# Layer norm by centring the activation and one accumulating variance pass, decay folded per 256 tokens, new prologue and drain

## The chip, the cores and the metric

The kernel runs on one core of a Trainium2 chip. The profile shows four compute engines: PE (TensorE, matrix products), DVE (VectorE), ACT (ScalarE) and POOL (GpSimd). They run side by side (busy for 91, 75, 69 and 66% of one span in the kernel before), each in the order in which the program queues its work. SP only issues DMA transfers here. The kernel keeps its tiles in two on-chip memories, SBUF and PSUM; it has the matrix products written to PSUM.

The metric is the device time of one execution in microseconds (us). Each kernel was run several times. The time of a run is about 1.8 us longer than the span that the profile shows.

## The reference, cut to what matters

```python
q, k, v: (8 batches, 8 heads, 576 tokens, 64)         # float32
rel = pos[:, None] - pos[None, :]
ret = scale * (q @ k.T) * where(rel >= 0, gamma[h] ** rel, 0)     # causal, decaying; no softmax
x = (ret @ v), all heads of a token side by side      # (4608 tokens, 512)
h = x @ w_in                                          # (4608, 1024)
sm = exp(h - max(h)) / sum(exp(h - max(h)))
solu = h * sm
ln = (solu - mean(solu)) / sqrt(var(solu) + 1e-6) * g_ln
out = ln @ w_out                                      # (4608, 512)
```

Two things make the code below easier to read. Layer norm does not change when solu is multiplied by a constant per token, so the kernel drops the division by the sum `se` of the exponentials and adds 1e-6 * se * se to the variance instead (`eps` in the changed kernel). And the attention is done in windows of 256 tokens (2 tiles of 128) with a running state, the decayed sum of k x v, for everything earlier.

## The kernel before: the parts that matter here

The work is 36 token tiles of 128 tokens (index `t`) and 36 half-windows of 4 heads (index `i`). Every operation is listed with its engine, what it needs and what buffers it takes; a list of queue orders per engine, worked out in advance, says in what order each engine runs them. So the program fixes the order of each engine's work, and `h`, the PSUM tile of the first product, has a single buffer.

POOL prepares the attention inputs and the state. All of these read SBUF:

```python
def scale(i, nm, base):                       # q and k: 128x512, times gamma ** position
    t = pools["qk16"].tile([P, 2, 4, D], F16, ...)
    nc.gpsimd.tensor_tensor(out=t..., in0=st[i][nm + "r"], in1=g_of(i, base), op=ALU.mult)
def cast_v(i):                                # v: 128x512
    nc.gpsimd.tensor_copy(out=t, in_=st[i]["vr"])
def state_b(i, c):                            # decay of the state, 128x128
    nc.gpsimd.tensor_tensor(out=d["g"][:, c], in0=d["tt"], in1=g128(i % 2), op=ALU.mult)
def state_cast(i):                            # state to fp16, needed by PE's xy product
    for e in range(2):
        nc.gpsimd.tensor_copy(out=s16[ee[e], :, :, ee[e]], in_=st[i]["g"][ee[e]])
```

The layer norm of a tile. Here `w2c16` is g_ln * w_out with its mean over the 1024 rows taken off once, in the prologue, so that solu itself need not be centred: the weights do it.

```python
def exp_(t):   # ACT; e and the sum of e
    nc.scalar.activation(out=d["e"], in_=d["h"], func=ACT.Exp, accum_out=ws[w]["se"][:, c : c + 1])
def solu(t):   # DVE
    nc.vector.tensor_tensor(out=d["solu"], in0=d["h"], in1=d["e"], op=ALU.mult)
def stats(t):  # DVE
    for half in range(2):
        nc.vector.bn_stats(out=bs[:, half], in_=tk[t]["solu"][:, half * 512 : half * 512 + 512])
    nc.vector.bn_aggr(out=d["mv"][:, c], in_=bs)
    if c:      # once for two tiles
        nc.vector.scalar_tensor_tensor(out=x, in0=d["se"], scalar=1e-6, in1=d["se"],
                                       op0=ALU.mult, op1=ALU.mult)
        nc.vector.tensor_tensor(out=d["x2"], in0=x, in1=d["mv"][:, :, 1], op=ALU.add)
def ln_tp(t):  # PE: 8 transposes of d["solu"], then ACT copies them to lnT
def mm2(t):    # PE: o_ps = sum over c of lnT[:, c].T @ w2c16[:, c]
def w_mean(c), w_center(x):   # prologue: mean of the weights by matmuls (PE), centring (DVE)
```

The softmax here doesn't subtract the row's maximum and nothing guards it: scores larger than these inputs give would overflow.

## Time and profile before

The time is 230.75 us (median of 3 runs, 229.46 to 231.84).

| part of the span (228.9 us) | reading | from |
|---|---|---|
| prologue | first products (L412) start at 19.2, 25.7, 34.9, 40.3 us; the first second product (L475) at 44.1 | starts of the groups in the timeline |
| steady part | one first product every 5.343 us, from the eighth (64.2) to the 33rd (197.7) | the same |
| drain | 17.4 us from the last first product (211.5) to the end | the same |

The busy times of the whole execution, from the page's first part (engine, us, share of the span, number of instructions):

```profile
PE 208.0 (91%) x2964; PEld 122.9 (54%) x2964; DVE 170.7 (75%) x307; ACT 157.6 (69%) x230; POOL 150.9 (66%) x243
```

The same by stretches of time (window view; columns as in its first line, each number in brackets a count of instructions):

```profile
core 0: us, PE busy (x) PEld busy (x) DVE busy (x) ACT busy (x) POOL busy (x), PEclk, DMA share, GB/s
0.00:25.00 25.00, 16.94 (x237) 9.28 (x238) 12.38 (x31) 11.47 (x17) 17.37 (x29) 0.80 0.98 277
25.00:50.00 25.00, 21.08 (x319) 12.39 (x318) 20.92 (x39) 18.14 (x27) 18.29 (x30) 0.93 0.99 280
...
125.00:150.00 25.00, 25.00 (x409) 15.59 (x407) 21.43 (x39) 19.32 (x29) 20.61 (x34) 1.00 0.74 204
150.00:175.00 25.00, 25.00 (x404) 15.45 (x403) 20.88 (x38) 19.43 (x30) 20.76 (x35) 1.00 0.68 180
```

In the steady part PE is busy all the time and nothing else is. DVE and POOL have about 4 of 25 us left each. The page's summary of the chain that ended last agrees (its share by engine):

```profile
PE 70%; DMA 9%; DVE 6%; POOL 5%; ACT 4%; SPq 2%; issue 2%; ACTq 0%; POOLq 0%; DVEq 0%
```

DVE's costliest groups (form, count, busy us, mean ns of one, then the idle time in front of them):

```profile
L438 DVE BATCH_NORM_STATS2 bs<-solu 128x6 f32<-128x512 f16 x72 | 46.0, 680 | 0.1
L432 DVE TENSOR_TENSOR solu<-h_ps,e_sb 128x1024 f16<-128x1024 f32 x36 | 44.0, 1223 | 20.8 <-ACT e_sb L425 20.8
L363 DVE TENSOR_TENSOR ret<-s_ps,masks 128x1024 f16<-128x1024 f32 x36 | 43.7, 1215 | 6.5 <-PE s_ps L330 6.4
```

Note that the large multiplies `solu` and `ret` have one input in PSUM, and that the statistics take one input (0.674 to 0.695 us in all 72). Only tiny instructions of this DVE queue have two inputs in SBUF. What becomes of such an instruction is in the timeline (start, duration, engine, line, what it does):

```profile
59.72 1.04 POOL L258 TENSOR_TENSOR k_1258<-kr,small 128x512 f16<-128x512 f32 x1 [0.27 <-DMA kr<-in_k_dram]
...
60.02 0.76 DVE L446 SCALAR_TENSOR_TENSOR w<-se 128x2 f32<-128x2 f32 x1
...
60.72 1.04 POOL L258 TENSOR_TENSOR q_1320<-qr,small 128x512 f16<-128x512 f32 x1
60.81 0.97 DVE L449 TENSOR_TENSOR w_1255<-w,mv 128x2 f32<-128x2 f32 x1
```

Each of the two DVE instructions handles two numbers per partition and takes 0.11 or 0.16 us when nothing holds it up.

### The profile page before, as it was taken

What the parts mean: (1) busy time and instruction counts of PE and PEld (TensorE: products, weight loads), DVE (VectorE), ACT (ScalarE), POOL (GpSimd) and SP (SyncE); (2) the same over time, 40 slices, a digit from 0 to 9 for tenths busy, and PEclk for the clock granted to TensorE, in tenths of its full rate; (3) what the DMA queues carried; (4) which work ended last, traced back from release to release, by engine and by line L of the source; (5) the groups of instructions that cost most, each with busy time, mean ns of one, the idle gap of its engine ahead of it and who ended that gap; (6) DMA issues with size and microseconds to landing.
All of it is one profiled execution on the core that took longest, in us unless ns stands there. A gap on an engine that the chain in (4) does not pass through costs nothing.

```text
span 228.9 us, 7317 instructions
## 1 busy us (share of the span) xinstructions
PE 208.0 (91%) x2964; PEld 122.9 (54%) x2964; DVE 170.7 (75%) x307; ACT 157.6 (69%) x230; POOL 150.9 (66%) x243
## 2 busy tenths in 40 slices
PE   7577587998989999999999999999999999999961
PEld 2344244565556665655666665666666656654420
DVE  6334778996888898987788798879898989676700
ACT  2165596677678777777777777777777777777621
POOL 3787549868786976978287978797697879201010
PEclk9857979999999999999999999999999999999999
DMA  7999999783992355999776866877855442222243
GB/s 189 329 351 254 299 316 289 207 244 77 282 333 61 103 128 135 272 312 296 196 203 180 210 185 184 240 212 196 224 128 132 122 98 66 63 57 49 47 102 83
DMA packets 66659, 42.64 MB, mean 186 GB/s; under 512 B 5056, under 2 KB 60480, under 8 KB 66624
## 3 DMA queue, kind: packets, MB, share of 16 engines
q1 hardware_dynamic: 66192, 41.96, 66.8%
q8 instruction: 23, 0.38, 0.7%
q10 hardware_dynamic: 432, 0.20, 0.4%
q14 instruction: 12, 0.10, 0.1%
HBM read 32.71 MB, written 9.44 MB: 184 GB/s over the span
## 4 chain that ended last, share of the span: by engine, by line
PE 70%; DMA 9%; DVE 6%; POOL 5%; ACT 4%; SPq 2%; issue 2%; ACTq 0%; POOLq 0%; DVEq 0%
PE o_ps L475 24%; PE h_ps L412 22%; PE xy L295 8%; DMA qr<-in_q_dram 6%; PE tln L461 6%; PE tqk L275 6%; PE s_ps L330 4%; DMA kr<-in_k_dram 3%; DVE solu L432 2%; DVE ret L363 2%; SPq L243 1%; POOL g L385 1%; DVE bs L438 1%; ACT o_sb L482 1%; ACT qkT L283 1%
## 5 line engine op out<-in xcount | busy, mean ns | idle before, releaser
L475 PE MATMUL o_ps<-w2c_120,lnT 128*128 128x512 f16 x288 | 68.3, 380 | 2.0 <-ACT o_sb L482 2.0
L412 PE MATMUL h_ps<-w_in_118,xT 128*128 128x512 f16 x288 | 68.6, 380 | 1.0 <-ACT w_in_118 L582 0.7
L432 DVE TENSOR_TENSOR solu<-h_ps,e_sb 128x1024 f16<-128x1024 f32 x36 | 44.0, 1223 | 20.8 <-ACT e_sb L425 20.8
L425 ACT ACTIVATE e_sb<-h_ps 128x1024 f32<-128x1024 f32 x36 | 36.8, 1024 | 20.5 <-PE h_ps L412 20.3
L363 DVE TENSOR_TENSOR ret<-s_ps,masks 128x1024 f16<-128x1024 f32 x36 | 43.7, 1215 | 6.5 <-PE s_ps L330 6.4
L438 DVE BATCH_NORM_STATS2 bs<-solu 128x6 f32<-128x512 f16 x72 | 46.0, 680 | 0.1
L283 ACT COPY qkT<-tqk 128x1024 f16<-128x1024 f16 x36 | 36.2, 1005 | 10.7 <-PE tqk L275 10.7
L412 PEld LDWEIGHTS <-xT 128*128 128x128 f16 x288 | 27.0, 98 | 27.9 <-issue 2.0
L475 PEld LDWEIGHTS <-lnT 128*128 128x128 f16 x288 | 25.7, 98 | 30.0 <-issue 2.6
L482 ACT ACTIVATE o_sb<-o_ps,rs 128x512 f32<-128x512 f32 x36 | 24.8, 688 | 23.7 <-PE o_ps L475 14.5
L469 ACT COPY lnT<-tln 128x1024 f16<-128x1024 f16 x36 | 36.2, 1004 | 1.8 <-PE tln L461 1.8
L385 POOL TENSOR_TENSOR g<-tt,small 128x128 f32<-128x128 f32 x48 | 19.6, 409 | 25.7 <-DVE tt L381 25.3
L461 PEld LDWEIGHTS <-solu 128*128 128x128 f16 x288 | 19.0, 99 | 8.3 <-DVE solu L432 0.8
L400 ACT CAST xT<-xy 128x512 f16<-128x512 f32 x36 | 21.4, 595 | 2.6 <-DVE g L377 1.5
L461 PE MATMUL tln<-ident,solu 128*128 128x128 f16 x288 | 22.5, 222 | 0.3 <-DVE solu L432 0.3
L381 DVE TENSOR_TENSOR tt<-xy,g 128x128 f32<-128x128 f32 x48 | 13.7, 286 | 7.6 <-ACT xT L400 3.8
L330 PE MATMUL s_ps<-qkT 64*64 64x128 f16 x576 | 15.6, 228 | 2.8 <-ACT qkT L283 2.8
L330 PEld LDWEIGHTS <-qkT 64*64 64x64 f16 x576 | 9.8, 110 | 6.2 <-ACT qkT L283 3.7
L377 DVE TENSOR_TENSOR g<-xy,small 128x128 f32<-128x128 f32 x16 | 4.6, 287 | 6.5 <-PE xy L295 4.8
L442 DVE BATCH_NORM_AGGREGATE mv<-bs 128x2 f32<-128x12 f32 x36 | 7.5, 209 | 1.2
L588 ACT ACTIVATE w2g_119<-w_f,gln 128x512 f16<-128x512 f32 x8 | 5.4, 716 | 2.5 <-DMA w_f<-in_moe_w_out_dram 2.4
L425 ACT ACTIVATION_READ_ACCUMULATOR e_sb<-h_ps 128x1 f32 x36 | 7.0, 194 | 0.0
(493 smaller groups left out, 292.7 us busy)
## 6 DMA issues: line engine op xcount, KB each, us to landing
kr<-in_k_dram SPq DMA_DIRECT2D x32, 256.0 KB, 4.7
vr<-in_v_dram SPq DMA_DIRECT2D x32, 256.0 KB, 4.7
qr<-in_q_dram SPq DMA_DIRECT2D x32, 256.0 KB, 4.2
out_dram<-o_sb SPq DMA_DIRECT2D x64, 128.0 KB, 2.5
w_in_f<-in_moe_w_in_dram SPq DMA_DIRECT2D x4, 512.0 KB, 7.5
w_f<-in_moe_w_out_dram SPq DMA_DIRECT2D x4, 512.0 KB, 7.9
qr<-in_q_dram SPq DMA_DIRECT2D x16, 64.0 KB, 2.1
kr<-in_k_dram SPq DMA_DIRECT2D x16, 64.0 KB, 2.0
```

Source lines behind the costliest of these rows:

```text
L283: nc.scalar.copy(out=d["qkT"], in_=d["tp"])
L330: nc.tensor.matmul(out=sv[ee[c], e, hp, j], lhsT=qkT[ee[e], 1, hp, j, ee[c]], rhs=qkT[ee[e], 0, hp, :, ee[c]], start=True, stop=True,)
L363: nc.vector.tensor_tensor(out=d["ret"].rearrange("p e h j q -> p (e h) (j q)"), in0=d["s"].rearrange("p e h j q -> p (e h) (j q)"), in1=ma ...
L385: nc.gpsimd.tensor_tensor(out=d["g"][:, c], in0=d["tt"], in1=g128(i % 2), op=ALU.mult)
L412: nc.tensor.matmul(out=h_ps[:, hh], lhsT=st[2 * w + dc // 2]["xT"][:, c, dc % 2], rhs=w_in16[:, dc, hh], start=(dc == 0), stop=(dc == 3),)
L425: nc.scalar.activation(out=d["e"], in_=d["h"], func=ACT.Exp, accum_out=ws[w]["se"][:, c : c + 1])
L432: nc.vector.tensor_tensor(out=d["solu"], in0=d["h"], in1=d["e"], op=ALU.mult)
L438: nc.vector.bn_stats(out=bs[:, half], in_=tk[t]["solu"][:, half * 512 : half * 512 + 512])
L461: nc.tensor.transpose(out=tp[:, c], in_=d["solu"][:, c * P : (c + 1) * P], identity=ident)
L469: nc.scalar.copy(out=d["lnT"], in_=d["tp"])
L475: nc.tensor.matmul(out=d["o"], lhsT=d["lnT"][:, c], rhs=w2c16[:, c], start=(c == 0), stop=(c == 7))
L482: nc.scalar.activation(out=d["osb"], in_=d["o"], func=ACT.Copy, scale=ws[t // 2]["rs"][:, t % 2 : t % 2 + 1])
```

## The change

The intent, as the code shows it: (1) The first second product is late because the weights must first be averaged (PE) and centred (DVE). So take that away, and centre the activation instead: DVE subtracts the mean from solu (`cen`). (2) The mean comes as a by-product of the solu multiply, and the variance from one pass cen x cen that accumulates, with eps as its start value, in place of two batch-norm statistics and their aggregate. (3) Fold the state's decay per 256 tokens, so POOL multiplies once instead of twice per half-window. (4) A new load order, filler products on PE up to the first second product, and the prologue's casts spread over the engines. (5) In the drain, two of the last second products use the score bank, and the last stores go out on two queues.

The core of the diff (cut):

```diff
@@ def exp_(t)
-        nc.scalar.activation(
-            out=d["e"], in_=d["h"], func=ACT.Exp, accum_out=ws[w]["se"][:, c : c + 1]
-        )
+        nc.scalar.activation(out=d["e"], in_=d["h"], func=ACT.Exp, accum_out=d["se"])
@@ def solu(t)
-        nc.vector.tensor_tensor(out=d["solu"], in0=d["h"], in1=d["e"], op=ALU.mult)
-    def stats(t):
-        ... two bn_stats, bn_aggr, and once for two tiles w and x2 (shown above)
+        nc.vector.tensor_tensor_reduce(
+            out=d["solu"], in0=d["h"], in1=d["e"], scale=1.0, scalar=0.0, op0=ALU.mult,
+            op1=ALU.add, accum_out=d["sum"],
+        )
+        nc.vector.scalar_tensor_tensor(
+            out=d["eps"], in0=d["se"], scalar=1e-6, in1=d["se"], op0=ALU.mult, op1=ALU.mult
+        )
+    def center(t):
+        nc.vector.tensor_scalar(
+            out=d["mu"], in0=d["sum"], scalar1=1.0 / DFF, scalar2=None, op0=ALU.mult
+        )
+        nc.vector.tensor_scalar(
+            out=d["cen"], in0=d["solu"], scalar1=d["mu"], scalar2=None, op0=ALU.subtract
+        )
+    def variance(t):
+        nc.vector.tensor_tensor_reduce(
+            out=junk, in0=d["cen"], in1=d["cen"], scale=1.0 / DFF, scalar=d["eps"], op0=ALU.mult,
+            op1=ALU.add, accum_out=ws[w]["var"][:, c : c + 1],
+        )
@@ ln_tp, mm2: PE transposes d["cen"]; rhs=w2g16 (not centred) in place of w2c16
@@ def state_a / state_b: one decay multiply per 256 tokens
-            nc.vector.tensor_tensor(out=d["g"][:, 0], in0=d["kv"][:, 0], in1=g128(hf), op=ALU.mult)
-    def state_b(i, c):
-        nc.gpsimd.tensor_tensor(out=d["g"][:, c], in0=d["tt"], in1=g128(i % 2), op=ALU.mult)
+            nc.vector.tensor_copy(out=d["g"][:, 0], in_=d["kv"][:, 0])
+    def state_b(i):
+        nc.gpsimd.tensor_tensor(out=d["g"][:, 1], in0=d["tt"], in1=g256(i % 2), op=ALU.mult)
@@ drain
+        if late(t):      # t in (NT - 4, NT - 2)
+            x = pools["s"].tile([P, 2, 2, 2, P], FP, tag="s", name="s_o")
@@ prologue: w_mean and w_center removed; g_ln loaded as 8 rows and transposed by PE;
   casts of weights, first q and v moved between DVE, ACT and POOL; new queue orders;
   filler products of zeros on PE where its queue has a gap, until the first M2
```

## The prediction

> **What bounds the kernel now.** Span 228.9 us in three parts.
> - Steady part. The chain of waits is PE alone from 63.6 to about 205 us, and the windows show PE busy 25.00 of 25 us at clock 1.00 from 75 to 200 us. First-product groups start 5.36 us apart. The change leaves PE's work per tile as it is: 5.36 us is the floor.
> - Prologue. First products start at 19.2, 25.7, 34.9, 40.3 us; the first second product (o_ps) only at 44.1, as it waits for all of w_out, its eight ACT scalings, eight mean matmuls (3.4 us) and eight DVE centrings (5.5 us). By then PE had done, at steady durations, about 17 us of lasting work: 27 us lost. Granted clock: 0.50 from 10 to 20 us.
> - Drain. From 216 us the last three second products alternate with one o_ps buffer's eviction: PE idle 1.10 and 0.90 us.
>
> **What the change does.**
> 1. Removes mean matmuls, centring and the 4-byte-element load of g (8.2 us to landing). By the new queue the last quarter of w_out is at 8.8 MB; at the trace's 320 GB/s that lands near 30 us, so I put the first second product at 31 to 33 us, behind three first products (about 13 us of lasting work). Loss there 18 to 20 us instead of 27: gain 7 to 9 us.[...]
> 2. Drain: alternating with the score bank removes the two waits (2.0 us); the longer solu, mean, centre chain puts back about 1 us before the last transposes; the last stores on two queues save about 1. Gain 2 to 3 us.
> 3. DVE per tile. Out: two batch-norm statistics (1.28 us), aggregate (0.21), half of w and x2 (0.15).[...] Net about +0.4: DVE goes from 4.5 (20.9 of 25 us busy) to about 4.9 of 5.36 us.
> 4. POOL loses 16 state multiplies (0.40 each).
> 5. Contention. [...]the tiny DVE add of L449 takes 0.16 us alone, 0.97 us beside POOL's scale of q (60.72 to 61.76). bn_stats did not do this; the new variance pass (two SBUF inputs) and centring will. POOL needs about 4.1 us per tile; with 1.2 to 1.5 us of lockout both POOL and DVE come near 5.36. I allow 0 to 5 us lost.
>
> **Sum.** 230.75 - 8 - 2.5 + 2.2 = 222.5 us, 8 in 10 between 215.5 and 229. Faster by over 2%: 0.75; within: 0.18; slower: 0.07.
>
> **What would show it.** First o_ps near 32 us; clock 1.00 from about 10 us; PE still solid with a 5.36 us period afterwards; no 1 us PE gaps in the last three second products; DVE 90% or more busy; POOL scales of q and k sometimes over 1.5 us and the variance pass over 1.3 us where they overlap.
>
> **What would make it wrong.** The lock saturating DVE or POOL: the period becomes 5.5 to 5.8 us and PE waits for scaled q/k, the mask or the centred tile, which eats the prologue's gain. Loads below 300 GB/s, leaving the first second product at 36 us or later. Fillers in front of ready work.

The total came to 222.5 us: 230.75, less 8 (prologue) and 2.5 (drain), plus 2.2 (contention). In point 3, with 1.64 us out and +0.4 net, what comes in had been put at about 2.0 us per tile, the author's estimate (measured later, undisturbed and from start to start: eps 0.12, centring 0.40, variance pass 1.20 us). The 1.2 to 1.5 us of lockout and the 2.2 us are estimates. What the trace of before had shown is that one tiny DVE instruction took 0.81 us longer beside POOL (0.97 against 0.16).

## The result, and the profile after

The changed kernel is correct and takes 238.58 us (median of 4 runs, 238.40 to 239.83). Ratios in this document are the mean time of one kernel's fast runs over the mean of the other's fast runs of the same rounds, so they are not quite the ratio of the quoted medians. Executions over 1.5% slower than the fastest of the same kernel are left out of the means. Here the ratio is 1.035, with a 95% interval of 1.029 to 1.042: slower, where the predicted time would be a ratio of 0.964 to the 230.75 us of before.

The starts of the first products say where the time went:

| part | before | after | difference |
|---|---|---|---|
| up to the eighth first product | 64.2 | 60.9 | -3.3 |
| the next 25 tiles (period 5.343 and 5.872) | 133.6 | 146.8 | +13.2 |
| the last three steps | 13.7 | 13.8 | +0.1 |
| last first product to the end | 17.4 | 15.2 | -2.2 |
| span | 228.9 | 236.7 | +7.8 |

So the prologue and the drain did get shorter, and the steady part, which was to stay as it was, took it all back. The page's busy times:

```profile
PE 210.1 (89%) x2993; PEld 122.4 (52%) x2993; DVE 205.2 (87%) x377; ACT 156.8 (66%) x228; POOL 171.9 (73%) x223
```

POOL has 20 instructions fewer than before and is busy for 21 us more. The windows, which answer to those of before:

```profile
0.00:25.00 25.00, 20.78 (x259) 10.21 (x262) 15.10 (x37) 11.26 (x17) 13.09 (x23) 1.00 1.01 306
25.00:50.00 25.00, 21.00 (x364) 12.41 (x352) 23.30 (x45) 18.11 (x27) 23.92 (x31) 1.00 1.06 283
...
125.00:150.00 25.00, 23.06 (x342) 13.82 (x341) 24.33 (x44) 17.31 (x26) 20.82 (x28) 1.00 0.64 172
150.00:175.00 25.00, 22.88 (x372) 13.95 (x371) 24.36 (x42) 17.84 (x27) 21.40 (x29) 1.00 0.67 180
```

PE is no longer solid: it idles 2 of 25 us. DVE is busy 24.3 of 25 us. The granted clock is 1.00 from the start, against 0.80 in the first 25 us before; the fillers were meant to bring this about, but no run tests whether they did. The chain has moved off PE:

```profile
PE 36%; POOL 28%; DVE 21%; issue 7%; ACT 5%; DMA 1%; POOLq 0%; SPq 0%; DVEq 0%; ACTq 0%
```

and PE's longest waits are for the cast state from POOL, 16.0 us in 22 waits over all its buffers. The two largest (what waited, for what: us in total, times, longest):

```profile
PE xy L295 <- POOL sbd_128 L397: 4.0, 4, 1.5
PE xy L295 <- POOL sbd_130 L397: 2.6, 3, 1.2
```

The new DVE groups of the layer norm:

```profile
L458 DVE CUSTOM_DVE_ANT_0 junk<-cen,eps 128x1024 f16<-128x1024 f16 x36 | 49.8, 1384 | 0.1
...
L451 DVE TENSOR_SCALAR cen<-solu,mu 128x1024 f16<-128x1024 f16 x36 | 33.7, 937 | 1.3
L440 DVE SCALAR_TENSOR_TENSOR eps<-se 128x1 f32<-128x1 f32 x36 | 15.6, 434 | 0.0
```

The centring takes 0.94 us on average, yet its shortest is 0.485; eps takes 0.43, its shortest 0.147. The timeline shows both near their longest (0.94 and 1.17 us; lines of the other engines left out):

```profile
134.16 1.04 POOL L258 TENSOR_TENSOR q_3047<-qr,small 128x512 f16<-128x512 f32 x1
134.33 0.08 DVE L436 DVE_READ_ACCUMULATOR2_ANT sum<- 128x1 f32 x1
134.33 0.88 DVE L440 SCALAR_TENSOR_TENSOR eps<-se 128x1 f32<-128x1 f32 x1
135.14 0.14 DVE L448 TENSOR_SCALAR mu<-sum 128x1 f32<-128x1 f32 x1
135.16 1.04 POOL L258 TENSOR_TENSOR k_3116<-kr,small 128x512 f16<-128x512 f32 x1
135.31 1.17 DVE L451 TENSOR_SCALAR cen<-solu,mu 128x1024 f16<-128x1024 f16 x1
```

Read it from the top. POOL starts its scale of q. The one-number eps multiply has two SBUF inputs; it starts a little later and ends together with it (135.21 and 135.20). POOL then starts the scale of k at once. The tiny mu has one input and is not held up (0.136 to 0.155 us in all 36). The centring comes 0.15 us after k has started and waits out all of it: it ends at 136.48, 0.28 us after k does. This is the pattern and not one case: in this trace 22 of the 36 eps multiplies took over 0.25 us, and every one of them ended within 0.02 us of the end of a POOL instruction; 24 of the 36 centrings took 1.04 us or more, and every one of them had started 0.15 to 0.29 us after a POOL instruction.

So the trace shows these DVE instructions waiting for POOL's, and how long: eps takes 0.147 us at its shortest and up to 0.94, the centring 0.485 and up to 1.17. eps has two inputs in SBUF; the centring has one tensor and a scalar per partition, and why it waits as well was not shown. It is also fast when alone: 0.485 us for 1024 elements, against 1.21 to 1.23 us for the solu multiply of as many, which has one input in PSUM.

The blocking goes the other way too. POOL's scale of q or k takes 1.03 to 1.05 us undisturbed and up to 2.02 us in this trace, and its cast of v took 1.48 us where it met the variance pass, against 0.61. From the timeline after:

```profile
98.80 1.40 DVE L458 CUSTOM_DVE_ANT_0 junk<-cen,eps 128x1024 f16<-128x1024 f16 x1
99.19 1.48 POOL L266 CAST v_2255<-vr 128x512 f16<-128x512 f32 x1
```

From 75 to 200 us, 16 casts of v start during a variance pass, and all take 1.48 us. The solu multiply is the same kind of instruction (CUSTOM_DVE_ANT_0), but has one of its inputs in PSUM: 20 scales of q start during it and take 1.03 to 1.05 us.

### The profile page after: what moved, and what is told of

It reads as the page before. It is cut to its first block, busy times and chain, and to the rows that moved or that the text cites. A ratio compares the mean times of both kernels' runs of the same rounds, so it can differ in the third digit from the quotient of the medians.

```text
span 236.7 us, 7458 instructions
## 1 busy us (share of the span) xinstructions
PE 210.1 (89%) x2993; PEld 122.4 (52%) x2993; DVE 205.2 (87%) x377; ACT 156.8 (66%) x228; POOL 171.9 (73%) x223
## 4 chain that ended last, share of the span: by engine, by line
PE 36%; POOL 28%; DVE 21%; issue 7%; ACT 5%; DMA 1%; POOLq 0%; SPq 0%; DVEq 0%; ACTq 0%
PE h_ps L415 12%; PE o_ps L494 10%; DVE solu L436 7%; PE xy L295 4%; ACT e_sb L428 4%; POOL g L388 3%; DVE junk L458 3%; DVE cen L451 3%; DVE ret L363 2%; PE tqk L275 2%; DVE eps L440 2%; PE wm L648 2%; PE s_ps L330 2%; POOL rs L467 2%; PE wm L641 2%
## 5 line engine op out<-in xcount | busy, mean ns | idle before, releaser
L436 DVE CUSTOM_DVE_ANT_0 solu<-h_ps,e_sb 128x1024 f16<-128x1024 f32 x36 | 43.9, 1219 | 7.1 <-ACT e_sb L428 7.1
L458 DVE CUSTOM_DVE_ANT_0 junk<-cen,eps 128x1024 f16<-128x1024 f16 x36 | 49.8, 1384 | 0.1
L451 DVE TENSOR_SCALAR cen<-solu,mu 128x1024 f16<-128x1024 f16 x36 | 33.7, 937 | 1.3
L388 POOL TENSOR_TENSOR g<-tt,small 128x128 f32<-128x128 f32 x32 | 13.5, 421 | 22.8 <-DVE tt L384 22.8
L467 POOL TENSOR_TENSOR rs<-var,small 128x2 f32<-128x2 f32 x18 | 12.3, 684 | 23.3 <-DVE var L458 23.2
L473 PEld LDWEIGHTS <-cen 128*128 128x128 f16 x288 | 18.6, 98 | 9.1 <-DVE cen L451 1.5
L473 PE MATMUL tln<-ident,cen 128*128 128x128 f16 x288 | 22.0, 220 | 1.0 <-DVE cen L451 1.0
L440 DVE SCALAR_TENSOR_TENSOR eps<-se 128x1 f32<-128x1 f32 x36 | 15.6, 434 | 0.0
L384 DVE TENSOR_TENSOR tt<-xy,g 128x128 f32<-128x128 f32 x32 | 9.3, 291 | 2.0
L648 PE MATMUL wm<-zeros 128*128 128x512 f16 x36 | 9.6, 381 | 0.0
```

The source lines that it names most:

```text
L436: nc.vector.tensor_tensor_reduce(out=d["solu"], in0=d["h"], in1=d["e"], scale=1.0, scalar=0.0, op0=ALU.mult, op1=ALU.add, accum_out=d["sum"],)
L451: nc.vector.tensor_scalar(out=d["cen"], in0=d["solu"], scalar1=d["mu"], scalar2=None, op0=ALU.subtract)
L458: nc.vector.tensor_tensor_reduce(out=junk, in0=d["cen"], in1=d["cen"], scale=1.0 / DFF, scalar=d["eps"], op0=ALU.mult, op1=ALU.add, accum_ ...
L473: nc.tensor.transpose(out=tp[:, c], in_=d["cen"][:, c * P : (c + 1) * P], identity=ident)
```

## The experiments

The theory after the result ("lock theory" in the expectations): the variance pass, the centring and eps on one side and POOL's instructions on the other hold each other up, and this, not the work, stretches the period. Rivals: DVE simply has too much work ("work theory"); the folded decay, the drain or the queue order does it; the longer chain from solu to the transposes does it. The labels b_two_port and b_one_port are only names here. "Period" below is always the mean distance of the first products from the eighth to the 33rd.

### The parts that have nothing to do with layer norm: b_drain and b_fold

```diff
# b_drain: before, with the new drain alone (score bank for t = NT-4, NT-2; last store on a second queue)
# b_fold: before, with the decay folded per 256 tokens alone (g256, one state_b, copy in place of the first multiply)
```

> The kernel before with the new drain alone (two of the last four second products into the score banks, last stores on two queues). From the traces: 17.4 us from the start of the last first product to the end before, less about 2.0 us of PE waits and up to 1 us of issue: 1.5 to 3 us faster, 228 to 229.5 us.

> The kernel before with the decay folded per 256 tokens alone: 16 POOL multiplications of 0.40 us gone, POOL busy 144 us instead of 151. POOL was not on the chain after 64 us: between 1.5 us faster and no change (229.5 to 231.5 us). Rival (the fold is what slows the changed kernel): 234 us or more.

b_drain took 228.04 us (ratio to before 0.988, 0.979 to 0.997), b_fold 228.91 us (0.992, 0.987 to 0.997). Each gives 2 to 3 us of gain by itself, and neither slows the steady part. So the loss is in the layer norm, or in what surrounds it.

### Is it POOL's presence? a_pool_light

```diff
# after, for i >= 6: POOL scales only a quarter of q and k into a scrap tile,
# and PE transposes a constant tile in its place (wrong result on purpose)
+        if i >= 6:
+            eng.tensor_tensor(out=qk_part, in0=st[i][nm + "r"][:, 0:1], in1=g_of(i, base)[:, 0:1], op=ALU.mult)
+            st[i][nm + "16"] = qk_fixed
+            return
```

> The changed kernel with POOL made light from the seventh half-window on: its q and k scalings handle a quarter of their elements into a scrap tile, PE transposes a constant tile instead (wrong result on purpose). DVE's program is untouched. Lock theory: centring falls from a median of 1.11 us to under 0.8, eps to under 0.25, period near 5.4 us, time 222 to 229 us. Work theory: DVE's instructions keep their durations and the time stays at 236 to 239 us.

222.24 us (0.961, 0.957 to 0.964), with a period of 5.326 us and PE solid again. DVE's instructions are all still there. The centring is back at its own length, over the 36 tiles (shortest, median and longest in ns):

```profile
L459 DVE TENSOR_SCALAR cen<-solu,mu x36: 485/487/845, 23.3 to 210.0; 128x1024 f16<-128x1024 f16 x36
```

So the changed kernel's DVE work by itself fits under PE's period, and the predicted time is what one gets when the centring and eps no longer wait. The rival "too much work" would have left the period where it was. (Not all of the contention is gone: the variance pass still takes 1.39 us on average, and POOL's cast of v 1.48 us in the median; POOL now has the time for that. So this run does not say that waiting for POOL's q and k scalings is the only cause.)

### What does extra DVE work cost in the kernel before? b_two_port and b_one_port

```diff
# both: before, with one useless DVE instruction per tile behind the solu multiply
+ b_two_port:  nc.vector.tensor_scalar(out=junk, in0=d["solu"], scalar1=0.5, scalar2=None, op0=ALU.mult)
+ b_one_port:  nc.vector.bn_stats(out=junk, in_=d["solu"][:, 0:352])
```

> The kernel before plus one useless tensor_scalar per tile, SBUF to SBUF, 128x1024 f16 (0.485 us alone, the shape of the centring pass). Lock theory: it takes about 1 us beside POOL and holds POOL up, DVE needs about 5.5 us per tile, time 233 to 239 us. Work theory: 4.5 + 0.45 us still fits in 5.36, time 230 to 232 us, the same as its twin with bn_stats.

> The kernel before plus one useless bn_stats per tile over 352 columns, about 0.5 us, which reads one SBUF input[...]. Both theories: 230 to 232 us, since DVE had 0.86 us to spare per tile. If it is as slow as the two-port twin, the lock theory falls.

b_two_port took 236.65 us (1.020, 1.015 to 1.026; period 5.548), b_one_port 234.92 us (1.014, 1.011 to 1.018; period 5.450). The second is a miss: the useless statistic takes 0.53 us on average and does not hold POOL up (scales of q and k 1.04 us, cast of v 0.61 on average), DVE seemed to have 0.8 us per tile to spare, and still it cost 1.4%. So the room that the busy share of before (21 of 25 us) suggests cannot all be used: from 75 to 200 us DVE idles 0.84 us per tile in before and still 0.54 in b_one_port, and yet the period has grown by 0.11. Which wait carries this I did not trace. The difference between the two kernels goes the way of the theory, but it is only 1.7 us. This pair does not settle the matter.

### eps by a pointer: a_eps_ptr

The multiply se * 1e-6 * se can also be written with se as a per-partition scalar in place of a second tensor.

```diff
-        nc.vector.scalar_tensor_tensor(
-            out=d["eps"], in0=d["se"], scalar=1e-6, in1=d["se"], op0=ALU.mult, op1=ALU.mult)
+        nc.vector.tensor_scalar(
+            out=d["eps"], in0=d["se"], scalar1=d["se"], scalar2=1e-6, op0=ALU.mult, op1=ALU.mult)
```

> The changed kernel, only eps = 1e-6*se*se written as tensor_scalar with se once as tensor and once as pointer scalar, so one SBUF tensor input instead of two. Lock theory[...]: eps falls from a median of 0.415 us to about 0.15; part of its wait moves to the centring pass behind it; first-product period 5.5 to 5.8 us instead of 5.87; time 230 to 237 us. Work theory (the added DVE instructions alone fill DVE): no instruction is taken away, 238 to 239 us.

235.72 us (1.019, 1.015 to 1.022), period 5.711, correct. eps now always takes 0.21 us (0.207 on average; 0.206 to 0.213 in all 36 of a_eps_bn, which has the same form): in this form no wait shows. A gain of about 3 us, but the kernel is still slower than before. What PE waits for is still the cast state, and POOL's casts are 1.5 times as long as undisturbed (0.40 and 0.61 us), which I put down to the variance pass (a_eps_bn, below, tests it). POOL's groups in a_eps_ptr (count, busy us, mean ns of one, idle before):

```profile
L397 POOL CAST sbd<-g 64x256 f16<-64x256 f32 x64 | 39.0, 610 | 3.3
L266 POOL CAST v<-vr 128x512 f16<-128x512 f32 x34 | 31.5, 927 | 1.6
```

### Back to the weights' centring after the prologue: c_hybrid6

```diff
# after, with eps by pointer; from tile 6 on the layer norm of before:
+        if t >= T0:   # T0 = 6
+            nc.vector.tensor_tensor(out=d["cen"], in0=d["h"], in1=d["e"], op=ALU.mult)   # not centred
+ ... variance by bn_stats and bn_aggr, second product with w2c16
+ ... w_mean (8 products), its copy to SBUF, and 8 w_center(x) put among the first tiles
```

> The changed kernel with the kernel before's layer norm from the seventh tile on: the weights are centred in the background (mean by eight matmuls before the first second product, one evicting copy, two centrings per tile behind tiles 2 to 5), later tiles use plain solu, bn_stats and the centred weights; eps once as tensor, once as pointer. New prologue, folded decay and drain stay. Lock theory: from tile 6 on period 5.33 to 5.40 us as before, PE solid; prologue gain of 3 to 5 us and drain gain of about 2 us remain: 222 to 227 us, faster than both. Rival (the new orders or the folded decay make the period longer): 234 us or more.

233.66 us (ratio 1.012): a miss of the total, but not of the mechanism. From 75 us on the period is 5.328 and PE is solid, as the theory said. By the trace the loss is in the transition: from 50 to 75 us PE is busy only 18.41 us (and DVE 24.58), and the eighth first product starts at 70.4 us (62.3 in a_eps_ptr). The eight centrings of weights, which now have two SBUF inputs (weights and mean), took 1.26 us on average there (0.74 in before, where the mean is in PSUM), and they stand in DVE's queue between the first tiles. What the steady part gained, the transition lost.

### The variance pass: a_eps_bn

```diff
# after, with eps by pointer, and
-        nc.vector.tensor_tensor_reduce(out=junk, in0=d["cen"], in1=d["cen"], ..., scalar=d["eps"], accum_out=var)
+        for half in range(2):
+            nc.vector.bn_stats(out=bs[:, half], in_=d["cen"][:, half * 512 : half * 512 + 512])
+        nc.vector.bn_aggr(out=mv, in_=bs)
+        nc.vector.tensor_scalar(out=var, in0=mv[:, 1:2], scalar1=d["eps"], scalar2=None, op0=ALU.add)
```

> The changed kernel with eps by pointer and the variance by bn_stats, bn_aggr and an addition by pointer[...]; DVE gets about 0.3 us more work per tile. Lock theory: POOL is no longer held up by the variance pass (its busy time falls from 172 to under 160 us), DVE's need is about 5.0 + 0.5 us: 231 to 236 us, at or below the 235.7 of the eps run. Work theory: more work, 238 us or more.

224.15 us (223.16 to 224.79), ratio to before 0.971 (0.965 to 0.976), correct. The expectation was wrong, by far: it had held the extra DVE work against this version, and the version is 11.6 us faster than a_eps_ptr. It beats both kernels. It keeps the changed kernel's queue orders, prologue, fold, drain and centring in front of the transposes, so none of these is what stretched the period. Its period is 5.370, PE is solid, and POOL is at 145.6 us busy instead of 171.9. DVE is busy for longer in it than in a_eps_ptr (195.3 against 193.3 us in all), and is busy 24 of 25 us in the steady part. The window from 125 to 150 us of a_eps_bn, to be read against those above (PE 25.00 before, 23.06 after):

```profile
125.00:150.00 25.00, 24.99 (x405) 15.42 (x403) 24.09 (x60) 19.17 (x29) 19.46 (x29) 1.00 0.75 204
```

POOL's casts are back at their own lengths, which bears out what was put down to the variance pass above (a_eps_bn, to be read against the two lines of a_eps_ptr):

```profile
L397 POOL CAST sbd<-g 64x256 f16<-64x256 f32 x64 | 25.3, 396 | 3.3
L266 POOL CAST v<-vr 128x512 f16<-128x512 f32 x34 | 21.6, 638 | 1.6
```

### Is it the second SBUF input, or the single long pass? a_var_one

```diff
# a_eps_ptr, with a pass of the same shape and with an accumulator, but one SBUF input
# (sum of the positive parts: wrong result on purpose)
+        nc.vector.tensor_scalar(out=junk, in0=d["cen"], scalar1=0.0, scalar2=None,
+                                op0=ALU.max, op1=ALU.add, accum_out=ss)
+        nc.vector.tensor_scalar(out=var, in0=ss, scalar1=1.0 / DFF, scalar2=d["eps"], op0=ALU.mult, op1=ALU.add)
```

> The changed kernel with eps by pointer, and the variance pass replaced by a DVE pass of the same shape with an accumulator but ONE SBUF input (sum of the positive parts of cen, 128x1024 into the same scrap tile), then one tiny scale-and-add. Wrong result on purpose. The two-input theory: as with the batch-norm version, period 5.33 to 5.42, median 222 to 227, the pass never over 1.45 us, POOL back to 143 to 150 us busy. Rival (one long pass with an accumulator read instead of two short statistics is what hurts, whatever its inputs): period 5.6 to 5.75, median 234 to 237, as with eps by pointer alone (235.72).

225.65 us (0.978, 0.973 to 0.982), POOL 145.1 us busy. The pass takes nearly the same time on DVE as the two-input one does undisturbed (1.27 us), and never more (all 36 of a_var_one; shortest, median and longest in ns):

```profile
L459 DVE TENSOR_SCALAR_CACHE_REDUCE junk<-cen x36: 1202/1208/1219, 29.6 to 212.9; 128x1024 f16<-128x1024 f16 x36
```

(The period, 5.452, is a little above what was expected.) So it is not the single long pass or its accumulator. The edit changes the kind of instruction too (from CUSTOM_DVE_ANT_0 to TENSOR_SCALAR_CACHE_REDUCE), but that is not it either: the solu multiply is of the first kind and neither waits (1.21 to 1.23 us in all 36 here) nor holds POOL up (above). What is left is the second SBUF input. One caution: "correct" in this document does not vouch for the variance.

### The same, in the kernel before: b_var_two

```diff
# before: two bn_stats and bn_aggr (1.49 us of DVE) replaced by one two-input pass
-        ... bn_stats x2, bn_aggr
+        nc.vector.tensor_tensor_reduce(
+            out=junk, in0=tk[t]["solu"], in1=tk[t]["solu"], scale=1.0 / DFF, scalar=0.0,
+            op0=ALU.mult, op1=ALU.add, accum_out=d["mv"][:, c, 1:2])
# mean square in place of the variance: slightly wrong on purpose
```

> The kernel before with one thing changed in its layer norm: the two batch-norm statistics and their aggregate (0.64 + 0.64 + 0.21 = 1.49 us of DVE per tile) become one accumulating pass solu x solu (the form of the changed kernel's variance pass, two SBUF inputs, 1.3 to 1.4 us plus an accumulator read of 0.08). The result is slightly wrong on purpose (mean square in place of variance). DVE's own work stays equal within 0.05 us per tile, so only the blocking of POOL differs. Theory (the long two-input pass holds POOL off for 1.3 us per tile): POOL, 4.2 us per tile before, cannot keep up with 5.34 us any more; period 5.5 to 5.75, PE below 24.7 of 25 us, median 235 to 241. Rival (it takes the changed kernel's centring, longer chain and fuller DVE together): period stays below 5.4 and median 229.5 to 232.

243.88 us (1.057, 1.051 to 1.062), more than the theory's range, with a period of 5.837. Nothing is centred here, and DVE is far from full: its busy time falls to 18.5 of 25 us, from 21. POOL carries the loss (POOL's state multiply, first before, then in b_var_two; shortest, median and longest in ns):

```profile
L385 POOL TENSOR_TENSOR g<-tt,small x48: 392/399/668, 9.9 to 193.3; 128x128 f32<-128x128 f32 x48
```

```profile
L386 POOL TENSOR_TENSOR g<-tt,small x48: 392/910/1382, 9.4 to 205.9; 128x128 f32<-128x128 f32 x48
```

The state multiply waits for the variance pass (24 of the 48 start during one and take 1.31 to 1.38 us, the other 24 take 0.39 to 0.51), the cast after it is late, and PE waits 12.5 us in all for the cast state. This one edit, which makes DVE's work no longer, costs 13 us, more than the whole change did. So neither a fuller DVE nor a longer chain is needed for such a loss.

### The other half: a_bn_only

```diff
# after, with the variance by bn_stats as in a_eps_bn, and nothing else: eps keeps its two SBUF inputs
```

> The changed kernel with the variance by batch-norm statistics of cen and nothing else: eps keeps its two SBUF inputs. It separates eps from the variance pass. If the variance pass alone is the cause: within 2 us of the version with both mended (224.15), so 223.5 to 226.5, period 5.35 to 5.42. If the tiny eps multiply also matters by itself (its wait for POOL adds 0.2 us per tile on a DVE that is 97% busy): 227 to 231, period 5.45 to 5.6.

236.70 us (1.025, 1.020 to 1.030), period 5.854. Both expectations were wrong. Mending the variance pass alone gains 2 us, mending eps alone 3 us, mending both 14.4 us (238.58 - 224.15). The two do not add up; each alone is enough to keep the kernel slow. POOL is undisturbed here (144.3 us busy). This time it is DVE that waits (DVE's groups in a_bn_only, over the whole execution; the numbers behind the count are busy us and mean ns of one):

```profile
L451 DVE TENSOR_SCALAR cen<-solu,mu 128x1024 f16<-128x1024 f16 x36 | 27.6, 767 | 1.3
L440 DVE SCALAR_TENSOR_TENSOR eps<-se 128x1 f32<-128x1 f32 x36 | 14.9, 415 | 0.0
```

To see what a tile costs on DVE, I took from the timeline, between 100 and 200 us, the mean distance from the start of each DVE instruction to the start of the next one. (The durations themselves overlap, by 0.08 us as a rule in the trace of after, so they cannot be added.) "Rest" is the measured period minus the lines above it:

| us per tile on DVE | after | a_eps_ptr | a_bn_only | a_eps_bn |
|---|---|---|---|---|
| eps | 0.48 | 0.12 | 0.42 | 0.12 |
| centring | 1.03 | 0.89 | 0.74 | 0.56 |
| variance (all its instructions) | 1.31 | 1.27 | 1.69 | 1.69 |
| then idle, until the exponential comes | 0.06 | 0.46 | 0.00 | 0.02 |
| rest | 2.99 | 2.97 | 3.00 | 2.98 |
| period | 5.872 | 5.711 | 5.854 | 5.370 |

The rest comes out the same in all four, as it should. Undisturbed, the first three would be 0.12 (eps by pointer), 0.40 and 1.20 us (the shortest distances in the trace of after). In the changed kernel, in a_bn_only and in a_eps_bn DVE issues without a pause: the period is DVE's sum. In a_eps_ptr DVE idles 0.46 us per tile; there the loop through POOL's blocked casts is what is slow.

### A try at less work: a_bn_mean

```diff
# eps by pointer; plain solu multiply; bn_stats and bn_aggr of solu give mean and variance; then the centring
# (the durations from which the queue orders are worked out are changed to match)
```

> A try at a better version, correct: eps by pointer, plain solu multiply, both mean and variance from batch-norm statistics of solu, then the centring. Against the batch-norm version (224.15) it takes away the accumulator read (0.08 us) and the mean multiply (0.15) per tile, and puts 1.5 us of statistics before the centring. If PE is the bound in the steady part the period stays 5.34 to 5.37; prologue and drain get up to 1.5 us longer each: 223 to 227 us. If a longer solu-to-transpose chain holds PE up: period over 5.45, 228 or more.

244.22 us (1.057, 1.051 to 1.063), correct and the slowest of all. DVE has less to do (21.5 of 25 us), but the statistics now stand between solu and the centring, and each part waits for the next: DVE idles 20.5 us in all for exponentials, PE waits 9.8 us for the cast state, 5.7 for the mask and 3.1 for the centring. It was meant as an improvement, and shows that a shorter list of work may be a longer loop. I did not take that loop apart any further, and the queue orders may differ too.

### Does eps do its harm by where it stands? a_bn_late

```diff
# a_bn_only, with the two-input eps moved from in front of mu and the centring to behind the mask,
# in front of the statistics
```

> The version with batch-norm variance and the two-input eps multiply (236.70 us; eps mean 0.415, centring 0.767), with eps moved from in front of the centring to behind the mask, in front of the statistics. Alignment theory (the tiny multiply ends when a POOL instruction ends, the next one starts then, and the centring 0.2 us later waits all of it out): centring back to 0.58 to 0.66 us, as with eps by pointer (0.617); eps itself 0.2 to 0.45; DVE saves 0.1 to 0.25 us per tile, median 228 to 233.5. Rival (where it stands makes no difference): centring 0.74 or more, median 235 to 238.

229.49 us (0.996, 0.994 to 0.999), 7 us less than a_bn_only for moving one instruction. Period 5.512. The same two groups as in a_bn_only, now in a_bn_late:

```profile
L448 DVE TENSOR_SCALAR cen<-solu,mu 128x1024 f16<-128x1024 f16 x36 | 22.0, 611 | 1.3
L455 DVE SCALAR_TENSOR_TENSOR eps<-se 128x1 f32<-128x1 f32 x36 | 9.7, 268 | 0.0
```

The centring is back at 0.61 us, as in a_eps_bn (0.62). This confirms the reading of the timeline above: the tiny multiply waits for POOL's instruction to end, which is the moment at which POOL starts its next one, and so the centring right behind it meets that one at its beginning. (In a_bn_only 13 of the 36 centrings take 1.17 us, and all 13 start 0.155 to 0.158 us after a POOL instruction.) But the gain is not the centring's alone: from start to start it gives 0.19 us per tile (0.74 to 0.55), and eps itself, which waits less in its new place, 0.26 (0.42 to 0.16), while the accumulator read that eps had covered now shows with 0.12.

### Is DVE time paid alike, work or wait? a_bn_junk and a_bn_junk2

```diff
# a_eps_bn with a useless statistic per tile
+ a_bn_junk:   between bn_aggr and the add:      nc.vector.bn_stats(out=junk2, in_=d["cen"][:, 0:176])
+ a_bn_junk2:  between bn_stats and bn_aggr:     nc.vector.bn_stats(out=junk2, in_=d["cen"][:, 0:320])
```

> The version with eps by pointer and batch-norm variance (224.15 us; DVE 24.0 to 24.3 of 25 us busy, period 5.37, equal to PE's) plus one useless batch-norm statistic of 176 columns per tile (one SBUF input, 0.35 to 0.37 us). If DVE sits exactly at the edge, so that any DVE time per tile, whether work or wait, is paid in full: 0.36 x 36 = 13 us, 234 to 238, period 5.65 to 5.75, and PE waiting for the cast state as in the kernel with the two-input eps (236.7, which has 0.36 us more DVE time per tile). Rival (plain work is absorbed; only waits for POOL hurt): 224 to 229.

a_bn_junk took 225.65 us (0.980), so by its number the rival was right. The trace says otherwise: the instruction was no addition. It ran in the pause between the aggregate and the add that needs it (DVE's timeline in a_bn_junk: start, duration, what):

```profile
143.06 0.21 DVE L463 BATCH_NORM_AGGREGATE mv<-bs 128x2 f32<-128x12 f32 x1
143.19 0.29 DVE L464 BATCH_NORM_STATS2 junk<-cen 128x6 f32<-128x176 f16 x1
143.39 0.20 DVE L465 TENSOR_SCALAR var<-mv,eps 128x1 f32<-128x1 f32 x1
143.51 1.22 DVE L437 CUSTOM_DVE_ANT_0 solu<-h_ps,e_sb 128x1024 f16<-128x1024 f32 x1
```

From the aggregate to the next solu it is 0.45 us here and 0.37 us without the useless instruction: 0.08 us were added, not 0.36. Hence the second version.

> The kernel of a_bn_junk was no clean test: its useless statistic stood between the aggregate and the add that depends on it, and ran mostly inside the gap that is there anyway (aggregate start to next solu 0.37 us without it, 0.45 us with it), so it added only 0.08 us per tile. Here a useless statistic of 320 columns stands right behind the two real ones, where DVE has no gap; at 0.60 us per 512 columns back to back it adds about 0.37 us per tile, about as much as the two-input eps multiply added with its waits (0.36 us; 236.7 us). If DVE stands at the edge in the 224.15 us version, so that work and waits are paid alike: period 5.62 to 5.75, median 233 to 238. If plain work is absorbed and only waits on POOL hurt: period below 5.5, median 224 to 229.

231.06 us (0.998, 0.992 to 1.004), period 5.592. It lies between the two expectations. By start-to-start distances the variance part grew from 1.69 to 1.94 us, so 0.25 us were really added, of which 0.22 show in the period. The expected 13 us had rested on 0.37. DVE time is thus paid almost in full in this kernel, whether it is work (here) or wait (a_bn_only): a_eps_bn stands at the edge, where DVE's sum (5.37) and PE's need (5.34) meet.

### Taking eps off DVE altogether: a_bn_act

```diff
# batch-norm variance; eps on ACT, right behind the exponential
+        nc.scalar.activation(out=d["eps"], in_=d["se"], func=ACT.Square, scale=1e-3)
```

> A try at the best version, correct: batch-norm variance, eps computed on ACT (Square of 0.001 x the exponentials' sum, straight after the exponential), so DVE has 0.21 us less per tile than in the 224.15 us version and ACT about 0.2 more of its 19 of 25 us. PE is then the bound with some room on DVE: period 5.34 to 5.36, DVE 23 to 23.5 of 25, prologue 0 to 1 us shorter: 222 to 224.5. If ACT's in-order queue holds PE up instead: 226 or more.

224.14 us (0.973, 0.971 to 0.976), period 5.371: equal to a_eps_bn. Nothing is gained: PE is the bound in both (24.98 of 25 us busy here). DVE, expected at 23 to 23.5 of 25 us, is at 24.0: the place of eps stays empty, since the mean multiply starts 0.12 us after the accumulator read even so. So a_eps_bn or this one is the version to keep: about 3% faster than before, and 6% faster than the change as given.

## Why the prediction was wrong, point by point

- **What bounds the kernel before: right.** PE was alone on the chain and solid in the steady part. "5.36 us is the floor" holds in a_pool_light, c_hybrid6, a_eps_bn and a_bn_act (5.33 to 5.37). a_var_one, at 5.452, is the exception: there PE still waits 4.7 us in all for the cast state, and why was not tested.
- **"Gain 7 to 9 us" in the prologue: the direction right, the size too large.** The first second product came at 34.4 us, not at 31 to 33. By the eighth first product the gain was 3.3 us; in a_eps_bn, without the two-input variance pass and eps, it was 6.1. So about 3 us of it were lost to contention, and the gain was put about 2 us too high besides. The clock's part came true: 1.00 from the start, against 0.80 in the first 25 us. (No run here takes the fillers alone away, so what they did for the clock is not shown.)
- **"Gain 2 to 3 us" in the drain: right.** 17.4 to 15.2 us; the new drain alone, in the kernel before, also gave about 2 to 3.
- **DVE per tile "about 4.9 of 5.36 us": about right.** Undisturbed, the table's figures give 0.12 + 0.40 + 1.20 + 2.98 = 4.70 us.
- **"POOL loses 16 state multiplies": right, and without harm** (b_fold).
- **Contention, "I allow 0 to 5 us lost", entered with +2.2: this is the step that failed.** That DVE and POOL would hold each other up was foreseen, and even the signs of it (the variance pass over 1.3 us, q and k over 1.5 us, a period of 5.5 to 5.8 us, against 5.87 measured); only what PE waits for, the cast state, was not on its list. But the term was about +13 in the steady part and +3 in the prologue, 16 us where 2.2 had been entered. Two errors lie in it. First, the text put 1.2 to 1.5 us of lockout beside POOL's 4.1 and let both engines "come near 5.36", yet it did not add waits to DVE's own 4.9. The measured waits of DVE are (0.48 - 0.12) + (1.03 - 0.40) + (1.31 - 1.20) = 1.10 us per tile, and 4.70 + 1.10 + 0.06 of idling is 5.86, the period within 0.02. Second, it counted the locks as one sum of holding times. But POOL's instructions got longer as well, while DVE waited: 83.6 us busy in the 100 us from 75 to 175, that is 4.91 us per tile (at 5.872 us a tile), against 76.0, or 4.08, in a_eps_bn. And the tiny eps multiply was not on the list of what would wait (it was counted as work alone), although the same kind of instruction had been read at 0.97 us in the trace of before. It held DVE for 0.36 us per tile beyond its work, and besides it lined up the centring with POOL's next instruction.
- **The chances, 0.75 for faster and 0.07 for slower, were too sure.** The prediction's own list of what would make it wrong had the right case at the top.

What stays open: how the two loops (DVE full of waits; POOL's casts held up by the variance pass) would divide the loss in the kernel as given cannot be told apart by single edits, since removing either leaves the other. And why b_var_two loses even more than the changed kernel was read from its trace (two state multiplies per half-window on POOL, each open to the block) but not tested.

## What to carry to other kernels

Before you replace a DVE instruction by another of equal length, count its SBUF inputs, and look at whether POOL reads SBUF in that time: one extra input in one instruction of 1.3 us cost this kernel 10 us (235.72 us in a_eps_ptr, 225.65 in a_var_one), and batch-norm statistics (0.667 to 0.696 us in all 72 of a_bn_only) or an accumulating one-input pass (1.202 to 1.219 us in all 36 of a_var_one) in its place did not. The count is not all: the centring has one tensor input and waited too (up to 1.17 us in the changed kernel), for a reason that was not shown; look at the trace. Add the waits to both engines, and compare the sum with the period of the engine that is the bound, from start-to-start distances and not from busy shares. Where two causes each hold the time up, mending one shows little; try both together before you drop either.
